# A new order by stored rules, output banks for the second batch's transform, zero fills by DMA, and the filter's sign applied once

## The chip, the cores and the metric

The kernel runs on one core of a Trainium2 chip. The metric is device time in microseconds (us) for one execution; lower is better. Times of the kernel before are the median of three runs. Engines are named as the trace does: PE is TensorE (PEld its weight loads), DVE is VectorE, ACT is ScalarE, POOL is GpSimd, SP is SyncE, which issues nearly all DMAs.

## The reference, cut to what matters

The input x has 8 batches of 3008 positions and 256 channels. Each batch is filtered in the frequency domain along its positions, and each of the 24064 resulting tokens goes through a two-layer network:

```python
X = np.fft.rfft(x, axis=1)
Y = X * (filt_r + 1j * filt_i)[None, :, :]
x = np.fft.irfft(Y, n=3008, axis=1).reshape(24064, 256)
h = x @ w_in                                  # 256 -> 2048
out = (h * (1.0 / (1.0 + np.exp(-1.702 * h)))) @ w_out   # 2048 -> 256
```

## The kernel before, in words

The transform of length 3008 = 64 x 47 is done as small matrix products: a 64-point step (`s1`), a 47-point step (`s2`), the product with the filter, and the way back (`i2`, `i1`). Values for the network are split into a rounded high half and a low half (`xh`, `xl`; `gh`, `gl`; the two halves of each weight), and three products of halves replace one.

Batch 0 is transformed by `first_fft` in plain float32; its filter rows (`f_s`, two frequency groups per DMA) are held in the tiles `f_y`, `f_o` (these in the pool `out`) and `f_buf`. The filter's imaginary part is scaled by a sign table, on ScalarE, in `filtered`. Batches 1 to 7 are transformed by `fft(b)`: `parts` splits x into halves, `s1` writes results into PSUM (kind "oz" in the output banks for the first two x tiles of batch 1), they go to memory (`a_d`), come back into the tile `zy` as z, and `forward`, `product`, `parted` and `backward` do the rest. `load_f` loads filter rows into `f_buf`; for batch 1 it loads them unsigned, scales them on ScalarE with a second sign table (`sign_sb`) and stores the signed rows to `fs` in memory, from which later batches load them.

The weights come as pairs of 32-bit words per number; `weight` turns each of 16 blocks (8 of w_in, 8 of w_out in turn) into halves with ScalarE, VectorE and GpSimd, in temporary tiles `w_tu`, over which `zy` is laid later. Token tiles 0 to 4 (512 tokens each, batch 0) are worked off in turns: `first_0` makes a first product (6 matmuls into an h bank, kind "l"), `gelu` its halves, `second_0` the second product (6 matmuls, added up in two output banks over a token tile's 16 turns). The first 32 turns go over token tiles 0 and 1 together, four turns for each pair of weight blocks. From then on, tokens are worked off in pairs of tiles, with seven products in place of eight: 7 batches of 3 pairs, 8 cycles each. `start`/`pair_signal` prepare the operands of the next pair while one is worked on.

PSUM has four banks "h" (first products, transform results) and four banks "o" (second products; transform results of kind "oz").

Nothing is issued as the code is read. The class `Planner` records every instruction with a cost in microseconds. `dues` gives each matmul a target time (the matmul costs summed in program order) and each other instruction a due time, counted back from the matmuls it feeds and from the tiles that must come free. `plan` then walks the five engines along simulated clocks: the engine whose clock is lowest takes, of what is ready and has room, the instruction with the lowest due (TensorE: the lowest target, within REACH of the lowest open one). VectorE and GpSimd exclude each other for work between SBUF tiles (`port`). The order that results is written out by hand for each engine, so that every engine works its list in that order and waits where it must. All instructions of the plan show the same line in the trace, so groups are told apart by their tiles. A tile's name there is that of the first user of its place: `half_of_xh` and `half_of_xl` are both places of the pool `half`, `tab_of_tab` becomes the pairs' c tile, `big_of_x` a tile of the pool `big`.

Places the change touches: `_tables` (sign tables), `Planner.dues`, `room`, `plan`; `nc.caps` (how many tiles of a kind are open at once); `filtered`; `load_f`, `forward` and `backward` in `fft`; and the loop over `turns` (`LEAD`, `BLANK`), which fills unused rows of `zy` and `c_buf` with zeros on GpSimd.

Of the kernel before, what the change touches and what calls it, by code (L numbers as in the profile page):

```python
# [20 lines left out]
P = 128  # L21
# [10 lines left out]
def _tables():  # L32
# [59 lines left out]
    sign_q, d_q, e_q = np.zeros((P, NG)), np.zeros((P, 2, 2, 48)), np.zeros((P, 2, 2, 48))  # L92
    row = np.arange(R).reshape(2, 2, NH)
    for u in range(2):
        h, q = slice(48 * u, 48 * u + 48), slice(64 * u, 64 * u + 48)
        sign_0[h] = sign_q[q] = sign[:, :, u]
# [11 lines left out]
    tabs = [t1_0, np.eye(P), d_0, sign_0, e_0, t2, t1_q, d_q, e_q, t2_q, sign_q]  # L108
# [125 lines left out]
class Planner:  # L234
# [7 lines left out]
    HOP, REACH, NEAR, AHEAD = 0.2, 30.0, 2.5, 50.0  # L242
# [103 lines left out]
    def dues(self):  # L346

        ops, before, lines = self.ops, {}, {}
        for n, o in enumerate(ops):
            for m in o.preds:  # L350
                ops[m].succs.append(n)
        for n, o in enumerate(ops):
# [9 lines left out]
        now, target = 0.0, {}  # L362
        for n, o in enumerate(ops):
            if o.eng == "tensor":
                target[n] = now
                now += o.cost
        for n in range(len(ops) - 1, -1, -1):
            o = ops[n]
            due = target.get(n, now + 20.0)
# [3 lines left out]
            o.due = due  # L373
        return target, now, {k: [t for t, _ in line] for k, line in lines.items()}

    def plan(self):
        ops = self.ops
        target, now, lines = self.dues()
        free = {k: {i: 0.0 for i, (_, after) in enumerate(v) if after is None} for k, v in self.sites.items()}
        turn = {k: 0 for k in lines}  # L380
        held = {k: [] for k in lines}
        left_of = {name: len(u) for name, u in self.users.items()}
        last = {}
        ready = {e: [] for e in self.ENGINES}
        clock = {e: 0.0 for e in self.ENGINES}
        port, pipe = 0.0, 0.0
        for n, o in enumerate(ops):
            o.left, o.at = len(o.preds), 0.0
            if not o.left:
                ready[o.eng].append(n)  # L390
        left, order, rank, head, done = len(ops), [], sorted(target), 0, set()
        first = {name: next((target[n] for n in u if n in target), 0.0) for name, u in self.users.items()}

        def opens(o):
            return [b for b in o.names.values() if isinstance(b, Block) and b.slot is None]

        def room(o, t):
            for b in opens(o):
                if lines[b.kind][turn[b.kind]] is not b:
                    return False  # L400
                if b.kind in self.caps and sum(last.get(k.name, 1e9) > t if not left_of[k.name] else 1 for k in held[b.kind]) >= self.caps[b.kind]:
                    return False
                if b.kind == "x" and here < 200 and o.due > here + self.AHEAD:
                    return False
                n = sum(v <= t + 1e-9 for v in free[b.pool].values())
                if b.kind == "f":
                    for k in "agbl":
                        if k in lines and turn[k] < len(lines[k]):
                            n -= first[lines[k][turn[k]].name] < here + self.NEAR
                if n < 1:  # L410
# [3 lines left out]
        while left:  # L414
            eng = min(self.ENGINES, key=lambda e: clock[e])
            t = clock[eng]
            while head < len(rank) and rank[head] in done:
                head += 1
            here = target[rank[head]] if head < len(rank) else 1e9
            best, soon, rival = None, 1e9, 1e9  # L420
            other = {"vector": "gpsimd", "gpsimd": "vector"}.get(eng)
            if other and clock[other] <= t + 1e-9:
                rival = min((ops[n].due for n in ready[other] if ops[n].port and ops[n].at <= t and room(ops[n], t)), default=1e9)
            for n in ready[eng]:
                o = ops[n]
                if o.at > t + 1e-9:
                    soon = min(soon, o.at)
                elif o.port and port > t + 1e-9:
                    soon = min(soon, port)
                elif o.port and rival < o.due:  # L430
                    soon = min(soon, t + 0.01)
                elif eng == "tensor" and target[n] > here + self.REACH:
                    pass
                else:
                    key = (target[n] if eng == "tensor" else o.due, n)
                    if (best is None or key < best[0]) and room(o, t):
                        best = key, n
            if best is None:
                clock[eng] = min(t + 0.05, soon)
                if t > 2 * now + 1000:  # L440
                    stuck = [ops[r] for q in ready.values() for r in q]
                    raise RuntimeError(f"stuck: {[(o.eng, o.call, list(o.names)) for o in stuck][:8]}")
                continue
            n = best[1]
            o = ops[n]
            ready[eng].remove(n)
            for b in opens(o):
                turn[b.kind] += 1
                b.slot = min((v, i) for i, v in free[b.pool].items())[1]
                del free[b.pool][b.slot]  # L450
                held[b.kind] = [k for k in held[b.kind] if left_of[k.name] or last[k.name] > t] + [b]
            clock[eng] = t + o.cost
            o.at, o.end = t, clock[eng] + o.extra
            if o.call == "dma_start":
                pipe = max(pipe, t + 1.5) + (o.extra - 3.2)
                o.end = pipe + 1.7
            if o.port:
                port = clock[eng]
            order.append(n)
            done.add(n)  # L460
            left -= 1
            for name, b in o.names.items():
                left_of[name] -= 1
                last[name] = max(last.get(name, 0.0), o.end)
                if isinstance(b, Block) and not left_of[name]:
                    free[b.pool][b.slot] = last[name] + self.HOP
                    for pool, i in self.opened_by.get(name, ()):
                        free[pool][i] = last[name] + self.HOP
            for m in o.succs:
                p = ops[m]  # L470
                p.left -= 1
                p.at = max(p.at, o.end + self.HOP if p.eng != eng or o.call == "dma_start" else clock[eng])
                if not p.left:
                    ready[p.eng].append(m)
        self.span = max(o.end for o in ops), now
        order.sort(key=lambda n: (ops[n].at, n))

        def real(a):
# [3 lines left out]
            return a.on(self.sites[b.pool][b.slot][0].on(b.dtype, b.name))  # L482

        for n in order:
            o = ops[n]
            getattr(getattr(self.nc, o.eng), o.call)(*map(real, o.args), **{k: real(v) for k, v in o.kw.items()})  # L486

# [10 lines left out]
def tile_kernel(  # L498
# [47 lines left out]
    nc.caps = {"first": 6, "w": 5, "ws": 2, "x": 2, "ab": 4, "raw": 4, "l": 2}  # L546
# [25 lines left out]
    sign_sb = const.tile([P, P], F32, name="sign_sb")[:, :NG]  # L572
# [124 lines left out]
    def first_fft():  # L697
# [29 lines left out]
        load_in(sign_sb, tabs[:, TAB + LATE + P :])  # L727
# [21 lines left out]
        def filtered(g):  # L749
# [5 lines left out]
            nc.scalar.activation(f[:, i, 1], f[:, i, 1], AF.Copy, scale=table["sign_0"][:R, g : g + 1])  # L755
            f_r, f_i = (f[:, i, c : c + 1].broadcast_to((R, 2, D)) for c in range(2))
# [26 lines left out]
    def fft(b):  # L783
# [80 lines left out]
        def forward(g, k):  # L864

            for u in range(2):
                ps = held(f"s2_{b}_{g}_{k}_{u}")
# [34 lines left out]
        def backward(i):  # L902
# [3 lines left out]
            for u in range(2):  # L906
                ps = held(f"i2_{b}_{i}_{u}")
# [257 lines left out]
    LEAD, NEXT, TAIL, AHEAD, BLANK = 24, 70, 20.0, 4, 28  # L1165
# [187 lines left out]
```

## Time and profile before

| what | value |
|---|---|
| median of 3 runs | 2294.06 us (2293.56 to 2294.53) |
| the profiled execution | 2293.91 us, of which the span of its instructions is 2292.1 us |
| mean granted TensorE clock | 0.995 of full |
| PE busy | 2251.4 us (98%), 10416 matmuls |
| DVE, ACT, POOL busy | 1483.2, 1638.0 and 1101.0 us (65, 71 and 48%) |
| DMA | 475.40 MB, mean 207 GB/s |

Busy time of an engine is the sum of its instructions' times; register, semaphore and DMA-issuing instructions are left out. PE is the busiest throughout, so the question at any place is what PE waits for there.

### The profile page before, as it was taken

The page shows a single profiled execution, that of the slowest core. Times are in us where ns is not written, and L with a number is a line of the kernel's source. Part 1 is how long each engine was busy: PE and PEld are TensorE (multiplying, and loading weights), DVE is VectorE, ACT ScalarE, POOL GpSimd, SP SyncE. Part 2 cuts the span into 40 slices and gives each one's busy share as a digit, 9 for nine tenths or more (in the row PEclk, how much of TensorE's full clock was granted, in tenths as well). Part 3 has the DMA queues.
Part 4 walks back from the last instruction along what each step waited for, and adds up shares of the span by engine and source line. Part 5 has one row for each costly group of instructions (what it writes and reads, how often), then busy time and mean ns, then how long its engine had stood idle before and what let it go on. Part 6 is the DMA issues. An engine that isn't in the chain of part 4 may idle for free.

```text
span 2292.1 us, 31503 instructions
## 1 busy us (share of the span) xinstructions
PE 2251.4 (98%) x10416; PEld 1866.8 (81%) x10416; DVE 1483.2 (65%) x2262; ACT 1638.0 (71%) x2939; POOL 1101.0 (48%) x941
## 2 busy tenths in 40 slices
PE   8699999999999999999999999999999999999999
PEld 8587788888888888888888888888888788888887
DVE  5857865778557874578755886457865678643433
ACT  6657967777767776677776877767777677766665
POOL 5654654565426654366453564435644456322211
PEclk9899999999999999999999999999999999999999
DMA  6736658866778568885688766887668776555443
GB/s 215 224 120 184 184 159 256 238 203 210 237 255 234 182 207 258 250 227 186 206 260 246 218 199 196 277 242 222 190 196 273 197 220 190 185 171 162 145 167 107
DMA packets 191907, 475.40 MB, mean 207 GB/s; under 512 B 19840, under 2 KB 91264, under 8 KB 191744
## 3 DMA queue, kind: packets, MB, share of 16 engines
q1 hardware_dynamic: 191600, 473.33, 67.1%
q8 instruction: 82, 1.34, 0.3%
q14 instruction: 81, 0.66, 0.1%
q10 hardware_dynamic: 144, 0.07, 0.0%
HBM read 367.94 MB, written 105.38 MB: 206 GB/s over the span
## 4 chain that ended last, share of the span: by engine, by line
PE 83%; DVE 2%; ACT 1%; issue 0%; POOL 0%; DMA 0%; POOLq 0%; ACTq 0%
PE bank_h L486 43%; PE bank_o L486 39%; DVE zy_of_zy L486 0%; DVE u_buf L486 0%; DVE tab_of_tab L486 0%; DVE big_of_x L486 0%; DMA wo_of_wo<-w 0%; ACT gh_of_gh L486 0%; DVE c_all L486 0%; POOL zy_of_zy L486 0%; DVE wi_of_br L486 0%; ACT c_all L486 0%; ACT bank_h L486 0%; DVE wo_of_wo L486 0%; ACT tab_of_tab L486 0%
## 5 line engine op out<-in xcount | busy, mean ns | idle before, releaser
L486 PE MATMUL bank_o<-wo_of_wo 128*128 128x512 f32 x2016 | 535.7, 390 | 0.0
L486 PE MATMUL bank_o<-gh_of_gh,wo_of_wo 128*128 128x512 f32 x1648 | 462.7, 392 | 3.3 <-DVE f_buf L486 3.3
L486 POOL TENSOR_TENSOR gl_of_gl<-tab_of_tab,gh_of_gh 128x512 fp32r<-128x512 f32 x168 | 218.1, 1298 | 497.4 <-ACT tab_of_tab L486 400.3
L486 PEld LDWEIGHTS bank_o<-wo_of_wo 128*128 128x128 f32 x2016 | 378.4, 188 | 77.7
L486 PE MATMUL bank_h<-y_a,wi_of_wi 128*128 128x512 f32 x1584 | 431.7, 392 | 2.1 <-DVE wo_of_wo L486 1.1
L486 PE MATMUL bank_h<-y_of_y,wi_of_wi 128*128 128x512 f32 x1464 | 415.1, 393 | 3.6 <-DVE big_of_x L486 2.5
L486 PEld LDWEIGHTS bank_o<-gh_of_gh,wo_of_wo 128*128 128x128 f32 x1648 | 309.3, 188 | 68.5 <-DVE f_buf L486 3.2
L486 PEld LDWEIGHTS bank_h<-y_a,wi_of_wi 128*128 128x128 f32 x1584 | 294.9, 188 | 65.1 <-DVE tab_of_tab L486 2.8
L486 ACT ACTIVATE bank_h<-bank_h 128x512 f32<-128x512 f32 x584 | 346.3, 593 | 0.3
L486 PEld LDWEIGHTS bank_h<-y_of_y,wi_of_wi 128*128 128x128 f32 x1464 | 273.5, 188 | 62.4 <-DVE big_of_x L486 4.0
L486 DVE TENSOR_TENSOR gl_of_gl<-bank_h,gh_of_gh 128x512 fp32r<-128x512 f32 x244 | 168.3, 690 | 214.2 <-ACT bank_h L486 208.6
L486 DVE TENSOR_TENSOR wo_of_wo<-bank_h,wo_of_wo 128x512 fp32r<-128x512 f32 x340 | 233.8, 688 | 80.5 <-ACT bank_h L486 68.0
L486 PE MATMUL bank_h<-wo_of_wo,wi_of_wi 128*128 128x512 f32 x960 | 268.6, 392 | 1.3 <-DVE tab_of_tab L486 0.7
L486 ACT ACTIVATE gh_of_gh<-bank_h 128x512 fp32r<-128x512 f32 x244 | 146.0, 598 | 168.7 <-PE bank_h L486 162.0
L486 PE MATMUL bank_o<-gl_of_gl,wo_of_wo 128*128 128x512 f32 x824 | 263.3, 393 | 1.6 <-POOL gl_of_gl L486 0.9
L486 ACT ACTIVATE wo_of_wo<-bank_h 128x512 fp32r<-128x512 f32 x340 | 201.0, 591 | 28.9 <-PE bank_o L486 15.8
L486 PEld LDWEIGHTS bank_h<-wo_of_wo,wi_of_wi 128*128 128x128 f32 x960 | 178.6, 188 | 39.3 <-DVE tab_of_tab L486 2.2
L486 ACT COPY wi_of_br<-bank_h 128x512 f32<-128x512 f32 (+1 forms) x242 | 141.8, 587 | 72.1 <-PE bank_h L486 66.6
L486 POOL TENSOR_TENSOR zy_of_zy<-u_buf,zy_of_zy 48x512 fp32r<-48x512 f32 x112 | 157.9, 1410 | 69.1 <-DVE zy_of_zy L486 58.3
L486 DVE TENSOR_TENSOR c_all<-bank_h,c_all 48x512 f32<-48x512 f32 x224 | 153.9, 687 | 48.0 <-ACT c_all L486 43.0
L486 PEld LDWEIGHTS bank_o<-gl_of_gl,wo_of_wo 128*128 128x128 f32 x824 | 154.1, 189 | 36.2 <-POOL gl_of_gl L486 3.4
L486 POOL TENSOR_TENSOR zy_of_zy<-c_buf,zy_of_zy 48x512 fp32r<-48x512 f32 x112 | 150.8, 1347 | 58.3 <-DVE zy_of_zy L486 32.9
(231 smaller groups left out, 3229.0 us busy)
## 6 DMA issues: line engine op xcount, KB each, us to landing
wi_of_wi<-w SPq DMA_DIRECT2D x168, 896.0 KB, 5.4
wo_of_wo<-w SPq DMA_DIRECT2D x168, 512.0 KB, 5.7
zy_of_zy<-a_d SPq DMA_DIRECT2D x224, 192.0 KB, 4.4
a_d<-big_of_x SPq DMA_DIRECT2D x110, 256.0 KB, 5.0
out_dram<-out_of_f_o SPq DMA_DIRECT2D x46, 512.0 KB, 6.7
f_buf<-fs SPq DMA_DIRECT2D x96, 192.0 KB, 3.5
big_of_x<-in_x_dram SPq DMA_DIRECT2D x30, 512.0 KB, 5.9
b_d<-big_of_x SPq DMA_DIRECT2D x62, 192.0 KB, 4.2
```

Source lines behind the costliest of these rows:

```text
L486: getattr(getattr(self.nc, o.eng), o.call)(*map(real, o.args), **{k: real(v) for k, v in o.kw.items()})
```

## The change

- The plan is made in steps of 25 us of simulated time. Each step has a rule from `POLICIES`: which copy of the due times is used (the plain ones or one of eight with normal noise of 1 to 8 us), NEAR and REACH. `WAYS` stores the rule of each of 91 steps, one character each; after them the plain rule goes on. The choice at each moment is as before (lowest due first).
- Due times have a further link: the users of the last four "oz" tiles come before the opening of the fourth output tile "o".
- Caps: "l" 3 instead of 2, and a new kind "of", 2.
- For batch 1, the results of `forward` and `backward` for u = 1 go to output banks (kind "of") instead of h banks.
- `filtered` stores its signed filter rows to `fs`, two groups at a time; `load_f` loads from `fs` for every batch; the scaling, the stores of batch 1 and the second sign table go.
- The unused rows 48 to 63 and 112 to 127 of `zy` are filled with zeros by two DMAs out of zero rows of `d_sb` at turn 24; the eight memsets of `zy` and the two of `c_buf` go.

```diff
-    HOP, REACH, NEAR, AHEAD = 0.2, 30.0, 2.5, 50.0
+    HOP, AHEAD, STEP, SIGMA = 0.2, 50.0, 25.0, (1.0, 1.0, 3.0, 3.0, 8.0, 1.0, 2.0, 2.0)
+    POLICIES = [(i, 2.5, 30.0) for i in range(9)] + [(i, near, reach) for i in (0, 1) for near, reach in ((1.0, 30.0), (4.0, 30.0), (2.5, 10.0), (0.0, 20.0))]
+    WAYS = "10683121a0744gg11801450a044ee55043a5e9eea200003ddee21000091eee241030ceee4e28a0013005078000"
...
+                if t.kind == "o" and len(line) == 4:
+                    for u, _ in lines.get("oz", [])[-4:]:
+                        for m in self.users[u.name]:
+                            before.setdefault(m, []).append(n)
...
+        due = np.array([o.due for o in ops])
+        rng = np.random.default_rng(0)
+        self.dues_of = [due.tolist()]
+        for sigma in self.SIGMA:
+            self.dues_of.append((due + sigma * rng.standard_normal(len(due))).tolist())
...
+        s, mark = self.ready_to_plan(), 0.0
+        for way in self.WAYS:
+            mark += self.STEP
+            self.go(s, self.POLICIES[int(way, 36)], mark)
+        assert self.go(s, self.POLICIES[0], 1e9)
+        self.emit(s)
...
-    nc.caps = {"first": 6, "w": 5, "ws": 2, "x": 2, "ab": 4, "raw": 4, "l": 2}
+    nc.caps = {"first": 6, "w": 5, "ws": 2, "x": 2, "ab": 4, "raw": 4, "l": 3, "of": 2}
...
             nc.scalar.activation(f[:, i, 1], f[:, i, 1], AF.Copy, scale=table["sign_0"][:R, g : g + 1])
+            if g % 2:
+                nc.sync.dma_start(fs[:, g - 1 : g + 1], f[:, i - 1 : i + 1])
...
             for to, of in at:
-                load_in(to, (fs if b > 1 else filt)[of])
-            if b == 1:
-                for n in range(2):
-                    m = 2 * g + n
-                    nc.scalar.activation(f[:, n, 1], f[:, n, 1], AF.Copy, scale=sign_sb[:Q, m : m + 1])
-                for to, of in at:
-                    nc.sync.dma_start(fs[of], to)
+                load_in(to, fs[of])
...
-                ps = held(f"s2_{b}_{g}_{k}_{u}")
+                ps = held(f"s2_{b}_{g}_{k}_{u}") if b > 1 or u == 0 else nc.tile("o", (P, 2, D), F32, f"s2_{b}_{g}_{k}_{u}", "of")
...
-            for c in c_buf[0:2]:
-                nc.gpsimd.memset(c[32:64], 0.0)
+            for r in (48, 112):
+                load_in(
+                    zy[0][r : r + 16].bitcast(F32).rearrange("p (n d) -> p n d", d=4 * P),
+                    d_sb[Q:, 0:4].bitcast(F32).rearrange("p a d -> p (a d)").rearrange("p (n d) -> p n d", n=1).broadcast_to((16, 8, 4 * P)),
+                )
...
-        if n >= BLANK and n - BLANK < 8:
-            r, j = divmod(n - BLANK, 4)
-            nc.gpsimd.memset(zy[0][32 + 64 * r : 64 + 64 * r, 1024 * j : 1024 * j + 1024].bitcast(F32), 0.0)
```

## Rows read from the trace of the kernel before

**Rows 1.** The page's first part: busy time, share, instructions of each engine.
```profile
PE 2251.4 (98%) x10416; PEld 1866.8 (81%) x10416; DVE 1483.2 (65%) x2262; ACT 1638.0 (71%) x2939; POOL 1101.0 (48%) x941
```

**Rows 2.** Busy time by stretch: length, then busy us (instructions) of each engine.
```profile
core 0: us, PE busy (x) PEld busy (x) DVE busy (x) ACT busy (x) POOL busy (x), PEclk, DMA share, GB/s
50.00:77.70 27.70, 24.31 (x133) 19.19 (x131) 26.49 (x41) 18.63 (x34) 16.81 (x15) 1.00 0.52 152
77.70:92.80 15.10, 0.35 (x2) 0.24 (x2) 14.74 (x18) 6.02 (x10) 9.93 (x8) 0.67 0.68 245
92.80:100.00 7.20, 4.67 (x11) 3.18 (x12) 5.88 (x8) 4.48 (x9) 5.50 (x4) 0.50 0.60 135
100.00:200.00 100.00, 99.66 (x459) 82.69 (x458) 60.23 (x108) 62.78 (x117) 49.81 (x40) 1.00 0.58 182
200.00:300.00 100.00, 95.07 (x415) 74.85 (x415) 81.79 (x121) 87.72 (x157) 64.11 (x60) 0.98 0.59 158
300.00:2250.00 1950.00, 1944.15 (x8907) 1613.73 (x8906) 1255.00 (x1909) 1404.30 (x2507) 925.42 (x776) 1.00 0.69 214
2250.00:2292.10 42.10, 37.57 (x166) 30.80 (x164) 14.03 (x21) 21.90 (x41) 5.17 (x4) 0.99 0.31 107
```

**Rows 3.** What PE waited for, whole span: us in total, times, longest.
```profile
PE bank_o L486 <- POOL half_of_xh L486: 14.7, 1, 14.7
...
PE bank_o L486 <- DVE f_buf L486: 3.3, 2, 2.5
```

**Rows 4.** POOL's timeline, 60 to 100 us: start, duration, instruction, idle before.
```profile
77.48 1.44 POOL L486 TENSOR_TENSOR wo_of_wo<-zy_of_w_tu,wo_of_wo 128x512 fp32r<-128x512 f32 x1
...
86.39 1.44 POOL L486 TENSOR_TENSOR wo_of_wo<-zy_of_w_tu,wo_of_wo 128x512 fp32r<-128x512 f32 x1
...
90.80 1.71 POOL L486 TENSOR_TENSOR half_of_xh<-out_of_f_o,half_of_xh 128x512 fp32r<-128x512 f32 x1
...
96.74 1.46 POOL L486 TENSOR_TENSOR wo_of_wo<-zy_of_w_tu,wo_of_wo 128x512 fp32r<-128x512 f32 x1
```

**Rows 5.** PE's timeline, 105 to 118 us: the first products of two turns.
```profile
109.04 1.52 PE L486 MATMUL bank_h<-y_of_y,wi_of_wi 128*128 128x512 f32 x6
...
111.76 1.52 PE L486 MATMUL bank_h<-y_of_y,wi_of_wi 128*128 128x512 f32 x6
```

**Rows 6.** POOL's timeline, 100 to 140 us: the next blocks of w_out.
```profile
112.29 1.29 POOL L486 TENSOR_TENSOR wo_of_wo<-zy_of_w_tu,wo_of_wo 128x512 fp32r<-128x512 f32 x1 [2.98 <-ACT wo_of_wo L486]
...
123.52 1.29 POOL L486 TENSOR_TENSOR wo_of_wo<-zy_of_w_tu,wo_of_wo 128x512 fp32r<-128x512 f32 x1
...
139.55 1.30 POOL L486 TENSOR_TENSOR wo_of_wo<-zy_of_w_tu,wo_of_wo 128x512 fp32r<-128x512 f32 x1 [1.49 <-ACT wo_of_wo L486]
```

**Rows 7.** What PE waited for from 100 to 300 us, the two longest.
```profile
PE bank_h L486 <- DVE big_of_x L486: 2.5, 3, 1.9
PE bank_h L486 <- DVE c_all L486: 1.7, 4, 0.7
```

**Rows 8.** Busy time of two short stretches, columns as in rows 2.
```profile
288.00:290.00 2.00, 1.94 (x5) 1.56 (x6) 1.79 (x4) 0.74 (x2) 1.43 (x1) 0.50 0.70 197
...
140.00:160.00 20.00, 20.00 (x96) 16.71 (x95) 8.38 (x21) 9.83 (x18) 13.46 (x13) 1.00 0.23 88
```

**Rows 9.** Two tiles' instructions: count, ns least/median/most, first and last start.
```profile
L486 ACT ACTIVATE f_buf<-f_buf,sign_sb x16: 492/508/511, 109.5 to 286.7; 112x256 f32<-112x256 f32 x16
...
L486 DVE COPY out_of_f_o<-bank_o x48: 425/692/693, 176.6 to 2288.0; 128x512 f32<-128x512 f32 x46, 128x256 f32<-128x256 f32 x2
```

**Rows 10.** DMA queue, 12 to 32 and 32 to 60 us: packets, MB, share.
```profile
q1 hardware_dynamic: 2281, 6.08, 103.1%
...
q1 hardware_dynamic: 1478, 2.63, 27.6%
```

**Rows 11.** POOL's timeline, whole span, its memsets: the run of eight.
```profile
142.16 7.75 POOL L486 MEMSET zy_of_zy<- 32x1024 f32 x8
```

**Rows 12.** What PE waited for from 300 us on, the longest single wait.
```profile
PE bank_h L486 <- POOL zy_of_zy L486: 1.0, 1, 1.0
```

More of the change, by code (lines that the diff above doesn't have):

```diff
@@ L351, in dues @@
                 ops[m].succs.append(n)
+            if o.eng == "tensor":
+                ideal[n] = now
+                now += o.cost
         for n, o in enumerate(ops):
@@ L372, in dues @@
                     due = min(due, ops[m].due - o.cost - o.extra - (self.HOP if ops[m].eng != o.eng else 0))
[L373 to L399, printed above, removed]
@@ new lines, in dues, with go, opens, room @@
+            o.due = due if due < 1e9 else self.last_due
+    def go(self, s, policy, mark):
+        ops, lines, target, rank = self.ops, self.lines, self.target, self.rank
+        shift, near, reach = policy
+        caps, first, ENGINES, HOP = self.caps, self.first, self.ENGINES, self.HOP
+        clock, ready, at, end, slot = s.clock, s.ready, s.at, s.end, s.slot
+        dues = self.dues_of[shift]
+        def opens(n):
+            return [b for b in self.blocks[n] if b.name not in slot]
+        def room(n, t):
+            for b in self.blocks[n]:
+                if b.name in slot:
+                    continue
+                k = b.kind
+                if lines[k][s.turn[k]] is not b:
@@ L400, in room @@
                     return False
-                if b.kind in self.caps and sum(last.get(k.name, 1e9) > t if not left_of[k.name] else 1 for k in held[b.kind]) >= self.caps[b.kind]:
+                if k in caps and sum(s.last.get(h.name, 1e9) > t if not s.left_of[h.name] else 1 for h in s.held[k]) >= caps[k]:
                     return False
-                if b.kind == "x" and here < 200 and o.due > here + self.AHEAD:
+                if k == "x" and here < 200 and dues[n] > here + self.AHEAD:
@@ L404, in room @@
                     return False
[L405 to L410, printed above, removed]
-                    return False
-            return True
-        while left:
-            eng = min(self.ENGINES, key=lambda e: clock[e])
+                m = sum(v <= t + 1e-9 for v in s.free[b.pool].values())
@@ L416, in plan @@
+                if k == "f":
+                    for j in "agbl":
+                        if j in lines and s.turn[j] < len(lines[j]):
+                            m -= first[lines[j][s.turn[j]].name] < here + near
+                if m < 1:
+                    return False
+            return True
+        idle = 0
+        while s.left:
+            eng = min(ENGINES, key=clock.__getitem__)
             t = clock[eng]
-            while head < len(rank) and rank[head] in done:
-                head += 1
@@ L431, in plan @@
                     soon = min(soon, t + 0.01)
-                elif eng == "tensor" and target[n] > here + self.REACH:
-                    pass
-                else:
[L435 to L438, printed above, removed]
+                elif eng == "tensor":
+                    if target[n] <= here + reach:
+                        todo.append((target[n], n))
+                else:
+                    todo.append((dues[n], n))
@@ L439, in plan @@
+            todo.sort()
+            n = next((n for _, n in todo if room(n, t)), None)
+            if n is None:
                 clock[eng] = min(t + 0.05, soon)
-                if t > 2 * now + 1000:
-                    stuck = [ops[r] for q in ready.values() for r in q]
-                    raise RuntimeError(f"stuck: {[(o.eng, o.call, list(o.names)) for o in stuck][:8]}")
+                idle += 1
+                if idle > 4000:
+                    return False
                 continue
-            n = best[1]
+            idle = 0
@@ L445, in plan @@
             o = ops[n]
             ready[eng].remove(n)
[L447 to L451, printed above, removed]
+            for b in opens(n):
+                s.turn[b.kind] += 1
+                free = s.free[b.pool]
+                slot[b.name] = i = min((v, i) for i, v in free.items())[1]
+                del free[i]
+                s.held[b.kind] = [k for k in s.held[b.kind] if s.left_of[k.name] or s.last[k.name] > t] + [b]
@@ L452, in plan @@
             clock[eng] = t + o.cost
-            o.at, o.end = t, clock[eng] + o.extra
+            at[n], end[n] = t, clock[eng] + o.extra
             if o.call == "dma_start":
-                pipe = max(pipe, t + 1.5) + (o.extra - 3.2)
-                o.end = pipe + 1.7
+                s.pipe = max(s.pipe, t + 1.5) + (o.extra - 3.2)
+                end[n] = s.pipe + 1.7
             if o.port:
[L458 to L461, printed above, removed]
+                s.port = clock[eng]
@@ L462, in plan @@
+            s.order.append(n)
+            s.done[n] = 1
+            s.left -= 1
+            s.work[eng] += o.cost
             for name, b in o.names.items():
[L463 to L466, printed above, removed]
+                s.left_of[name] -= 1
+                s.last[name] = max(s.last.get(name, 0.0), end[n])
+                if not s.left_of[name] and isinstance(b, Block):
+                    s.free[b.pool][slot[name]] = s.last[name] + HOP
@@ L467, in plan @@
                     for pool, i in self.opened_by.get(name, ()):
-                        free[pool][i] = last[name] + self.HOP
+                        s.free[pool][i] = s.last[name] + HOP
             for m in o.succs:
                 p = ops[m]
-                p.left -= 1
-                p.at = max(p.at, o.end + self.HOP if p.eng != eng or o.call == "dma_start" else clock[eng])
-                if not p.left:
+                s.wait[m] -= 1
+                at[m] = max(at[m], end[n] + HOP if p.eng != eng or o.call == "dma_start" else clock[eng])
@@ L474, in plan, with ready_to_plan @@
+                if not s.wait[m]:
                     ready[p.eng].append(m)
-        self.span = max(o.end for o in ops), now
-        order.sort(key=lambda n: (ops[n].at, n))
+        return True
+    def ready_to_plan(self):
+        ops = self.ops
+        self.target, now, before, self.lines = self.links()
+        self.last_due = now + 20.0
+        self.dues(self.target, before)
+        self.rank = sorted(self.target)
+        self.blocks = [[b for b in o.names.values() if isinstance(b, Block)] for o in ops]
+        self.first = {name: next((self.target[n] for n in u if n in self.target), 0.0) for name, u in self.users.items()}
+        due = np.array([o.due for o in ops])
[3 more added lines that the diff above has]
+            self.dues_of.append((due + sigma * rng.standard_normal(len(due))).tolist())
+        return State(self)
@@ L478, in real, with plan, emit @@
+    def plan(self):
+        s, mark = self.ready_to_plan(), 0.0
[4 more added lines that the diff above has]
+        self.emit(s)
+    def emit(self, best):
+        ops, at, order = self.ops, best.at, best.order
+        order.sort(key=lambda n: (at[n], n))
         def real(a):
@@ L481, in real @@
             b = a.tensor
-            return a.on(self.sites[b.pool][b.slot][0].on(b.dtype, b.name))
+            return a.on(self.sites[b.pool][best.slot[b.name]][0].on(b.dtype, b.name))
         for n in order:
@@ L486, in plan, with __init__ @@
             getattr(getattr(self.nc, o.eng), o.call)(*map(real, o.args), **{k: real(v) for k, v in o.kw.items()})
+class State:
+    def __init__(self, p):
+        ops = p.ops
+        self.free = {k: {i: 0.0 for i, (_, after) in enumerate(v) if after is None} for k, v in p.sites.items()}
+        self.turn = {k: 0 for k in p.lines}
+        self.held = {k: [] for k in p.lines}
+        self.left_of = {name: len(u) for name, u in p.users.items()}
+        self.last, self.slot = {}, {}
+        self.ready = {e: [] for e in p.ENGINES}
+        self.clock = {e: 0.0 for e in p.ENGINES}
+        self.port, self.pipe, self.work = 0.0, 0.0, {e: 0.0 for e in p.ENGINES}
+        self.wait = [len(o.preds) for o in ops]
+        self.at, self.end = [0.0] * len(ops), [0.0] * len(ops)
+        self.done, self.left, self.head, self.order = bytearray(len(ops)), len(ops), 0, []
+        for n, o in enumerate(ops):
+            if not self.wait[n]:
+                self.ready[o.eng].append(n)
 class Stream:
```

48 lines of the change are left out of this document (25 added, 23 removed).

## The prediction

> **What bounds the kernel now.** I read the page's first part, then the busy time by stretch, then who TensorE waited for, and last the timelines of the worst stretch. The first shows TensorE busy for 2251.4 of 2292.1 us [rows 1]: no edit changes what it has to multiply, so only its 40.7 us of idle and its stretches at half clock can be won. The second shows where they lie [rows 2]. From 300 to 2250 us only 5.85 us of 1950 are idle, and the last 42.1 us hold 4.53 (the last product's tail). The loss is at the start: 3.39 us idle from 50 to 77.7, 14.75 from 77.7 to 92.8, 2.53 from 92.8 to 100, 4.93 from 200 to 300. After the long gap the granted clock is 0.50, which is 1.2 of 2.4 GHz, and the 4.67 us of work to 100 us cost 2.34 us more than at full clock. So the stretch from 77.7 to 100 us loses 14.75 + 2.53 + 2.34 = 19.6 us.
>
> The waits name it [rows 3]: one wait of 14.7 us for a GpSimd write to `half_of_xh`, then f_buf. The write is the low half of the second batch's second x tile, issued by `parts`. GpSimd began it at 90.80, behind the conversion of weights (77.48 and 86.39 are two of those) [rows 4], and TensorE went on as it ended. Behind that matmul, in TensorE's written order, stand the second products of the first token tiles: until this transform result is copied out, it holds one of the four output banks, and the two token tiles of the first turns need all four. The f_buf wait is that copy. So one late low half blocks the turns, though their weights are there.
>
> **The change, part by part.** The sum starts from the profiled execution's own 2293.91 us (span 2292.1 and 1.8 around it), 0.15 below the median 2294.06.
>
> *The order, first 100 us.* New is a link in the due times: every user of the last four "oz" tiles (transform results in output banks, their copies among them) is now due before the fourth output tile opens. Beside it `l` goes from 2 to 3, so one more first product may wait for its gelu. And the plan runs in steps of 25 us, each with one of 17 rules (noise on the due times, NEAR, REACH); the first hundred microseconds have rules 1, 0, 6, 8. If the low half comes before the weights, what is late next? The weights. Four turns use one pair of weight blocks; a turn takes 2.72 us (109.04 to 111.76) [rows 5], so a pair lasts 10.9. The second block of a pair is complete (start plus duration) at 78.92, 87.83 and 98.20 [rows 4], then at 113.58, 124.81 and 140.85 [rows 6]. Walking on from 77.7: wait 1.2; work to 89.8, 100.7, 111.6; wait 2.0, to 124.5; wait 0.3, to 135.7; wait 5.1. That is 8.6 us of new waits, so 19.6 - 8.6 = 11.0 are won if weights come when they do now. GpSimd is busy 49.8 of 100 us from 100 to 200 [rows 2], so they could come earlier: at best only the first 1.2 remain, 18.4 won. At worst the low half is late again: 0, or as much as the gap once more in another place. I take 11.0, the end worked out from the present arrivals.
>
> *Second transform in output banks too.* Half of `forward`'s and `backward`'s results (u = 1) of the second batch go to "of" tiles, at most two. Today they share the four h banks with the first products, and from 100 to 300 us TensorE waits 2.5 us for `big_of_x` and 1.7 for `c_all` [rows 7], both copies of such results. Gain at most the 4.93 idle plus half of the 1.94 us that ran at 0.50 [rows 8]: 5.9. Against it: a token tile that opens its output banks may now find them held. There are three such changes (tile 2 to 3, 3 to 4, 4 to the pairs), each worth one copy, 0.69 us by VectorE [rows 9], behind another, say 1.3: 3.9 lost at worst. I take the two named waits, 4.2 won.
>
> *Sign once.* Gone are 16 ScalarE scalings of 0.508 us, 8.1 us in all [rows 9], 16 stores and the load of the sign table; the filter is now stored signed from the first batch, eight stores of 96 x 4 KB. ScalarE is busy 87.7 of 100 us from 200 to 300 [rows 2], and its share of the relief is in the 4.2 above. The eight stores go into SP's queue in the first 50 us, ahead of loads of weights and x. Together 3.1 MB; the queue moves 6.08 MB in the 20 us from 12 to 32 and is full there (103%), so they are worth 10.3 us of queue. From 32 to 60 it is used to 27.6% [rows 10], 20 us free. I charge nothing, since that cover is twice the need; without it every weight pair is up to 10.3 us later and TensorE pays that. The x loads into the `out` tiles now also wait for two of these stores to land; their first matmuls wait for the split table anyway.
>
> The Trainium skill (DMA: Bandwidth & Descriptors, "Issuing engines are not separate DMA queues") says that all transfers end up on the same 16 engines and interleave. By that rule the stores are no free filler, they slow the weight loads around them; the sum with all of it uncovered would be 10.3 us higher. The full queue from 12 to 32 us agrees, the free one after it limits it.
>
> *Zero fills.* Eight GpSimd memsets, 7.75 us in one run from 142.16 [rows 11], become two DMAs of zeros (16 rows of 16 KB each); two short ones vanish. TensorE is busy for all 20 us from 140 to 160 [rows 8]: nothing won. The DMAs must land before the second transform reads z: I charge nothing, TensorE having its turns meanwhile; a late one delays that transform once, by at most the 10.3 us of a full queue.
>
> *The other 1990 us.* Their work is the same, their order is newly chosen. Idle there is 5.85 us before the tail, so no more can be won; I take 0.
>
> Sum: 2293.91 - 11.0 - 4.2 = 2278.7, so 2279. Its own range is 2271 (7.4 more, weights earlier) to 2286.
>
> **The rivals.**
> *A. The gap stays or moves.* For: GpSimd took the low half after the weight blocks although x had long landed, and the shared rules of choice are the old ones; the link adds mostly to the copies, and the low half's due time was early before. VectorE is busy 26.5 of 27.7 us from 50 to 77.7 [rows 2], so the stretch has little slack for any order. Against: the copies are what holds the banks, and a step that stalls TensorE is what a choice among rules would avoid. Time: only the banks' part, 2293.91 - 4.2 = 2289.7, with a spread of 4.
> *B. Slower: the hand-overs.* 21 times (7 batches of 3) the signal of the next pair must be finished by GpSimd and VectorE just before its first product. Now the longest wait after 300 us is one of 1.0 [rows 12]; the rest are below it. Rules with noisy due times, kept for 25 us each, may make the last split late at each: 21 x 1.0 = 21 us. With the start's gain kept, 2278.7 + 21 = 2299.7; it is slower than before from 0.73 us a hand-over on. For: the plan's clock knows no queueing of DMAs beyond one pipe, and an order that is tight there has nothing left on the chip. Against: the present order, made by the same clock, loses next to nothing.
> *C. Nothing of it acts.* The noise is small and ties decide, so the order stays in essence: 2293.9 within 3.
>
> **How the numbers follow.** Forecast 0.57, A 0.20, B 0.15, C 0.08. What this kernel's measurement can tell from no change is 0.2%, 4.6 us: faster is below 2289.5, slower above 2298.6. Forecast gives faster 0.56, same 0.01; A is split evenly, 0.10 faster and 0.09 same, 0.01 slower; B gives 0.02, 0.02, 0.11; C 0.01, 0.05, 0.02. That is 0.69, 0.17 and 0.14; I shift 0.04 to slower for mishaps not listed: 0.66, 0.16, 0.18. The range goes from 2264 (most of the 18.4 and of the banks' 5.9) to 2298, up to B's lower half.
>
> **What would show it.** Right: no wait of TensorE over 5 us between 60 and 100 us, the low half of x done before the weight blocks, a granted clock of 1.00 there, and less than 2 us idle from 200 to 300. The weights' part is right if small waits for wi and wo stand at 110 to 145. Wrong: a wait of over 10 us for any x half or f_buf (A); more than 15 us idle from 300 to 2250, spread over the hand-overs (B); weight loads of the first 32 us that land some 10 us later than now (the stores).

## The result, and the profile after

The changed kernel takes 2260.82 us (median of 4 runs, 2260.01 to 2261.07) against 2293.81 for the kernel before, taken with it: ratio 0.9856, 95% interval 0.9839 to 0.9873. That is 33 us, where 15 were forecast; it lies 3 us below the range's low end.

The first part of the page after answers to [rows 1]:

```profile
PE 2240.7 (99%) x10416; PEld 1864.8 (83%) x10416; DVE 1469.7 (65%) x2262; ACT 1626.6 (72%) x2923; POOL 1093.2 (48%) x931
```

The number of matmuls is the same. Busy time by stretch, the stretches of [rows 2] up to 300 us:

```profile
50.00:77.70 27.70, 26.82 (x148) 21.57 (x147) 25.38 (x38) 20.14 (x38) 19.02 (x14) 1.00 0.64 191
77.70:92.80 15.10, 15.10 (x69) 12.49 (x68) 13.46 (x21) 11.03 (x21) 7.63 (x6) 1.00 0.58 200
92.80:100.00 7.20, 7.20 (x33) 5.99 (x32) 4.52 (x9) 4.55 (x9) 3.68 (x3) 1.00 0.53 178
100.00:200.00 100.00, 98.74 (x462) 81.74 (x462) 69.43 (x118) 69.49 (x127) 48.49 (x40) 1.00 0.64 179
200.00:300.00 100.00, 98.47 (x453) 79.96 (x452) 79.78 (x121) 82.80 (x150) 65.28 (x61) 1.00 0.54 150
```

From 77.7 to 100 us TensorE never rests, at a granted clock of 1.00; 19.6 us were lost there. From 50 to 77.7 it rests 0.88 us (3.39 before), from 200 to 300 it rests 1.53 (4.93 before, and about 1.6 more were lost at half clock from 288 to 292 us). On GpSimd, the low halves of x now stand ahead of all weight blocks but the first (59.57); answering to [rows 4] and [rows 6], its timeline from 50 us:

```profile
53.22 2.51 POOL L524 TENSOR_TENSOR half_of_xl<-out_of_f_o,half_of_xh 128x512 fp32r<-128x512 f32 x2
55.77 2.60 POOL L524 TENSOR_TENSOR half_of_xh<-out_of_f_o,half_of_xl 128x512 fp32r<-128x512 f32 x1
...
59.57 1.29 POOL L524 TENSOR_TENSOR wi_of_wi<-zy_of_w_tu,wi_of_wi 128x512 fp32r<-128x512 f32 x1
60.81 1.32 POOL L524 TENSOR_TENSOR half_of_xh<-out_of_f_o,half_of_xl 128x512 fp32r<-128x512 f32 x1
...
64.12 1.47 POOL L524 TENSOR_TENSOR wo_of_wo<-zy_of_w_tu,wo_of_wo 128x512 fp32r<-128x512 f32 x1
...
75.79 1.53 POOL L524 TENSOR_TENSOR wo_of_wo<-zy_of_w_tu,wo_of_wo 128x512 fp32r<-128x512 f32 x1 [1.30 <-ACT wo_of_wo L524]
...
87.25 1.52 POOL L524 TENSOR_TENSOR wo_of_wo<-zy_of_w_tu,wo_of_wo 128x512 fp32r<-128x512 f32 x1 [1.30 <-ACT wo_of_wo L524]
...
98.94 1.29 POOL L524 TENSOR_TENSOR wo_of_wo<-zy_of_w_tu,wo_of_wo 128x512 fp32r<-128x512 f32 x1 [3.52 <-ACT wo_of_wo L524]
...
108.49 1.81 POOL L524 TENSOR_TENSOR wo_of_wo<-zy_of_w_tu,wo_of_wo 128x512 fp32r<-128x512 f32 x1 [1.37 <-ACT wo_of_wo L524]
...
122.23 1.28 POOL L524 TENSOR_TENSOR wo_of_wo<-zy_of_w_tu,wo_of_wo 128x512 fp32r<-128x512 f32 x1
...
133.89 1.29 POOL L524 TENSOR_TENSOR wo_of_wo<-zy_of_w_tu,wo_of_wo 128x512 fp32r<-128x512 f32 x1
```

What came at 90.80 is done by 62.1, and the weights lose little by it. The second blocks of the pairs that the prediction walked along end at 77.3, 88.8, 100.2, 110.3, 123.5 and 135.2, where it had 78.9, 87.8, 98.2, 113.6, 124.8 and 140.9: the second and third 0.9 and 2.0 us later, the others 1.3 to 5.7 us earlier. TensorE's waits for weight blocks from 50 to 200 us (total, times, longest):

```profile
PE bank_h L524 <- ACT wi_of_wi L524: 0.3, 1, 0.3
```

Where else did time go? To compare equal work I use two marks of the SP timeline: the first store of the first pair's tokens (451.65 before, 425.87 after) and the first store of the last pair but one (2208.85 and 2175.15). Between them both kernels run 8019 matmuls, and from the second mark to the end of the span it takes 83.25 us in both. The span is 33.7 us shorter (2292.1 and 2258.4). So 25.8 us are won ahead of the first mark, and 33.7 - 25.8 = 7.9 between the marks, in work that the change does not touch. Before:

```profile
451.65:2208.85 1757.20, 1751.65 (x8019) 1453.62 (x8019) 1149.20 (x1744) 1271.64 (x2268) 846.20 (x711) 1.00 0.69 214
```

and after:

```profile
425.87:2175.15 1749.28, 1746.77 (x8019) 1454.14 (x8019) 1143.53 (x1745) 1270.15 (x2267) 845.08 (x711) 1.00 0.69 215
```

The idle between them fell only from 5.55 to 2.51 us, 3.0 of the 7.9. The other 4.9 stood in the busy column: the same 8019 matmuls count 1751.65 and then 1746.77. A matmul is shown as 0.39 us long, but in a run the next begins 0.227 us later (1.52 us for six), so about the first 0.16 us of every wait hides under the modelled end of the last matmul. The waits at the weight loads show more: 16.5 us in all before and 7.1 after, 9.4 less, somewhat over the 7.9 that were won. Between the marks, the four longest of ten groups before (us in total, times, longest):

```profile
PEld bank_h L486 <- DVE tab_of_tab L486: 5.0, 9, 0.6
PEld bank_h L486 <- DVE wo_of_wo L486: 3.8, 5, 1.0
PEld bank_o L486 <- POOL gl_of_gl L486: 3.4, 6, 1.2
PEld bank_h L486 <- POOL zy_of_zy L486: 1.5, 1, 1.5
```

and after, all there are:

```profile
PEld bank_h L524 <- DVE tab_of_tab L524: 3.1, 5, 0.9
PEld bank_h L524 <- DVE wo_of_wo L524: 2.6, 4, 0.9
PEld bank_h L524 <- DVE big_of_x L524: 1.4, 2, 0.9
```

### The profile page after: what moved, and what is told of

Its sections match the earlier page's. It is cut to its first block, busy times and chain, and to the rows that moved or that the text cites. A ratio compares the mean times of both kernels' runs of the same rounds, so it can differ in the third digit from the quotient of the medians.

```text
span 2258.4 us, 31563 instructions
## 1 busy us (share of the span) xinstructions
PE 2240.7 (99%) x10416; PEld 1864.8 (83%) x10416; DVE 1469.7 (65%) x2262; ACT 1626.6 (72%) x2923; POOL 1093.2 (48%) x931
## 5 line engine op out<-in xcount | busy, mean ns | idle before, releaser
L524 PE MATMUL bank_o<-wo_of_wo 128*128 128x512 f32 x2016 | 542.7, 390 | 0.0
L524 ACT COPY wi_of_t<-bank_h 128x512 f32<-128x512 f32 (+1 forms) x217 | 127.4, 587 | 87.1 <-PE bank_h L524 85.1
L524 POOL TENSOR_TENSOR zy_of_zy<-u_buf,zy_of_zy 48x512 fp32r<-48x512 f32 x112 | 152.9, 1365 | 72.5 <-DVE zy_of_zy L524 54.4
L524 DVE TENSOR_TENSOR c_all<-bank_h,c_all 48x512 f32<-48x512 f32 x208 | 142.4, 687 | 45.5 <-ACT c_all L524 42.0
```

## The experiments

Times are medians; the ratios of the numbered runs are to the kernel before on the same chip (2295.0 to 2295.6 there). The stored string has 90 characters, not the 91 that earlier parts speak of. "First mark" and "between" are as above.

| run | us | ratio (95%) | first mark | between |
|---|---|---|---|---|
| before | 2293.81 | 1 | 451.65 | 1757.2 |
| changed | 2260.82 | 0.9856 (0.9839-0.9873) | 425.87 | 1749.3 |
| 1 half first | 2286.16 | 0.9954 (0.9936-0.9972) | 442.48 | 1757.1 |
| 2 banks | 2276.31 | 0.9913 (0.9897-0.9930) | 433.90 | 1757.3 |
| 3 less work | 2281.33 | 0.9934 (0.9916-0.9952) | 438.35 | 1756.7 |
| 4 rules to 400 us | 2268.25 | 0.9879 (0.9861-0.9897) | 424.49 | 1758.5 |
| 5 one rule | 2268.26 | 0.9880 (0.9866-0.9895) | 430.10 | 1752.1 |
| 6 one rule, no "of" | 2269.31 | 0.9889 (0.9874-0.9903) | 431.34 | 1752.3 |
| 7 noisy rule | 2293.12 | 0.9991 (0.9982-1.0001) | 445.27 | 1762.9 |
| 8 rules chosen anew | 2253.55 | 0.9817 (0.9802-0.9831) | 421.96 | 1747.2 |
| 9 sign only | 2285.98 | 0.9959 (0.9945-0.9972) | 439.36 | 1761.0 |
| 10 l 3 only | 2286.38 | 0.9962 (0.9948-0.9975) | 442.22 | 1761.4 |
| 11 changed again | 2258.96 | 0.9840 (0.9826-0.9853) | 425.06 | 1749.4 |
| 12 as 8, again | 2253.51 | 0.9819 (0.9806-0.9832) | 421.50 | 1747.2 |

Runs 1 to 4 were on one chip, runs 5 to 8 on a second, runs 9 to 12 on a third. The stretch of runs 4 and 9 between the marks holds 5 and 10 matmuls more than the others' 8019 or 8020, 1.1 and 2.3 us of work.

**1. The low half first.**
```diff
             o.due = due
+            if any(name.startswith(("xh_1_0", "xl_1_0", "xh_1_1", "xl_1_1")) for name in o.names):
+                o.due = -50.0
```


> The kernel before, with one thing changed in the planner: the splits of the first two x tiles of batch 1 get the earliest due time of all, so GpSimd takes their low halves as soon as they can be made. Everything else, work, banks and caps, stays. Theory order (the gap is only the low half standing behind the weight blocks on GpSimd): the 14.7 us wait goes, the stretch from 77.7 to 100 us loses less than 4 us, and the time is 2294 less 11 to 18, so 2276 to 2283; losses from 200 us on stay as before. Rival banks (the first turns lack PSUM room, the half is only where it shows): the gap turns up elsewhere before 130 us and the time stays at 2290 or above.

The long wait is gone: TensorE waits 0.4 us for an x half, and the loss from 50 to 100 us falls from 23.1 to 6.3 (4.76 idle, 1.56 by the clock). What is late next is what the prediction named, the weights (waits of TensorE from 50 to 200 us):

```profile
PE bank_o L488 <- POOL wo_of_wo L488: 2.4, 3, 1.2
PE bank_o L488 <- ACT wo_of_wo L488: 1.3, 3, 0.5
...
PE bank_o L488 <- POOL half_of_xh L488: 0.4, 1, 0.4
```

9.2 us are won by the first mark. That is close to the 11.0 of the prediction, but partly by luck: the waits for weight blocks are 3.7 us (2.4 and 1.3), not 8.6, and the stretch from 300 to 450 us, which was to stay as before, now rests 2.9 us in place of 0.3. The time is 3 us above the expectation's upper end (9.5 us under the kernel before on its chip, 11 to 18 expected). The order caused the gap; moving the half alone does not give the whole 19.6 back.

**2. Caps and output banks alone.**
```diff
-    nc.caps = {..., "l": 2}
+    nc.caps = {..., "l": 3, "of": 2}
-                ps = held(f"s2_{b}_{g}_{k}_{u}")
+                ps = held(f"s2_{b}_{g}_{k}_{u}") if b > 1 or u == 0 else nc.tile("o", (P, 2, D), F32, f"s2_{b}_{g}_{k}_{u}", "of")
...
```


> The kernel before with the caps and banks of the change alone: l 3 instead of 2 and the second batch's u = 1 results in output banks. Rule of choice, link, sign, stores and memsets as before. Theory order: longer chains through held banks are what made the weights due early; with more room their due times fall behind those of the x halves, the gap closes (under 2 us lost from 77.7 to 100) and the 200 to 300 us stretch loses under 3 us instead of 6.4: 2266 to 2274. Rival rules (the stored rules close the gap): the 200 to 300 us stretch improves by 3 to 4 us, the gap stays above 8 us, time 2286 to 2291.

17.8 us are won by the first mark (25.8 in the changed kernel), with no stored rule and no link. The gap closes (2.2 us idle from 50 to 100), and 200 to 300 us rests 2.1. But 300 to 450 us now rests 6.0 us, where before it was 0.3, so the time is 2 us above the expectation:

```profile
50.00:100.00 50.00, 47.77 (x242) 39.56 (x242) 41.65 (x68) 35.82 (x67) 27.55 (x23) 1.00 0.66 200
...
300.00:450.00 150.00, 144.03 (x655) 116.52 (x654) 91.23 (x153) 105.76 (x190) 83.91 (x69) 1.00 0.83 254
```

The due times explain why the gap closes. `dues` counts back through held tiles (a tile's users are due before the opener of the tile that takes its place), and with two "l" tiles and one chain of "f" tiles that chain is longer than the matmuls' own time. Worked out from the kernels' code, the last low half of the two x tiles is due at 51.6 simulated us in the kernel before, in this run and in the changed kernel. In the kernel before, the low halves of seven weight blocks are due ahead of it (19.8 to 47.1). With the caps and banks of this run, and in the changed kernel, none is (52.0 and later). Each engine works its written list, so this is the order on the chip: in this run GpSimd has made that half by 60.1 us. The caps also change when a tile may open; no run parts the two effects.

**3. The removed work alone.**
```diff
 (filtered, load_f and the zero fills as in the change; caps, banks, rule and due times as before)
```


> The kernel before with the removed work alone: sign applied once and stored from batch 0, zero fills by two DMAs, the table and the memsets gone; banks, caps and the rule of choice as before, no link. Theory hidden (the removed work lay beside TensorE's): within 4 us of before, 2290 to 2296, the gap of 14 us still there. Rival draw (the gap is an accident of one order, and any edit that changes the order a little removes it): the gap is under 5 us, 2275 to 2282. The eight stores of the signed filter cost nothing if the first 50 us lose 4 to 5 us as before, and up to 10 us more if they hold up the weights.

The rival had it: 13.3 us by the first mark, although the rule and the caps are the old ones. The low half still comes behind weights, as the due times are those of the kernel before, but at 75.99 us in place of 90.80. The first 50 us rest 4.37 us (4.34 before): the eight stores cost nothing.

**4. Stored rules for 400 us only.**
```diff
-    WAYS = "10683121a0744gg11801450a044ee55043a5e9eea200003ddee21000091eee241030ceee4e28a0013005078000"
+    WAYS = "10683121a0744gg1"
```


> The changed kernel with the stored rules for its first 16 steps (400 us) only, the plain rule after them. The first 400 us are the same order. Theory rules (what the changed kernel gained from 450 us on, some 8 us, comes from the chosen rules): 2267 to 2271, the 8 us lost between 450 us and the end. Rival (the steady part gained by work removed or by the hand-over from the first 400 us): 2259 to 2263.

The first 400 us are as in the changed kernel, and between the marks the whole 7.9 us are lost again (1758.5, or 1757.4 for equal work):

```profile
424.49:2183.03 1758.54, 1752.30 (x8024) 1454.21 (x8024) 1147.36 (x1746) 1274.22 (x2271) 846.28 (x711) 1.00 0.70 214
```

So the steady part was won by the rules of choice and by nothing else in the change.

**5 and 6. One rule, with and without the output banks.**
```diff
-    WAYS = "10683121a0744gg1..."
+    WAYS = "a" * 91          # run 5: NEAR 4.0; run 6 also takes "of" out of forward and backward
```


> The changed kernel with one rule for all 91 steps: the plain due times, REACH 30, NEAR 4.0 in place of 2.5. Nothing is chosen per step. Theory rules (the stored string earns some 8 us in the first 400 us and 8 after): 2272 to 2278. Rival NEAR (one wider NEAR would have done it, the string is hardly needed): 2261 to 2268, of which the part after 450 us loses at most 3 us against the changed kernel.

> As the run with one rule (NEAR 4.0 throughout), but the second batch's u = 1 results go to the h banks again; l stays at 3. Theory banks (the output banks relieve the stretch from 100 to 300 us, as the prediction had it, about 4 us): 3 to 8 us slower than the one-rule run, lost between 50 and 300 us. Rival (the banks matter through the due times alone, and the token tiles' openings pay for them): within 2 us of the one-rule run.

Run 5 lies at the upper end of its rival: the change with one wider NEAR, nothing chosen, gets 26.8 us (2295.03 to 2268.26) of the 33 to 36 that the changed kernel gets, and 5 of the 8 between the marks:

```profile
430.10:2182.16 1752.06, 1748.31 (x8019) 1453.58 (x8019) 1130.89 (x1745) 1268.69 (x2268) 847.74 (x711) 1.00 0.69 214
```

Beyond it, the string is worth 6 to 9 us by the ratios (0.9880 against 0.9856 and 0.9840); in the traces it is 4.2 by the first mark and 2.8 between. Run 6 is the same as run 5 within its interval, and 1.2 us later at the first mark. In detail the output banks do relieve the stretch that the prediction had in mind (50 to 300 us rests 4.8 us with them, 7.8 without), but 300 to 450 us pays: it rests 4.6 with them and 1.1 without. What the banks relieve there is largely paid later.

**7. A rule with much noise.**
```diff
+    WAYS = "5" * 91          # due times with normal noise of 8 us
```


> The changed kernel with one rule for all steps, the one with the largest noise on the due times (normal, 8 us). Theory handovers (the slower rival of the prediction: noisy due times bring waits at the hand-overs all along): 15 to 30 us are lost after 300 us against the changed kernel, the time is 2285 to 2305, and the waits stand on the signal's splits. Rival (due times have slack, noise is harmless): 2262 to 2272.

Between the marks 13.6 us are lost against the changed kernel (5.7 against the kernel before), and ahead of the first 19.4. The time is inside the expectation, and the 13.6, with 2.6 us more rest from 300 us to the first mark, reach the low end of its 15 to 30. But the place is not the one expected: TensorE waits for the gelu's low halves (`gl`, and `wo`, where `gl` tiles lie later) and for the sums in the c tile (`tab`), not for the signal's splits. The three longest groups of waits at the weight loads between 445 and 2208 us:

```profile
PEld bank_o L524 <- POOL gl_of_gl L524: 7.2, 10, 1.6
PEld bank_h L524 <- DVE wo_of_wo L524: 3.0, 3, 1.3
PEld bank_h L524 <- DVE tab_of_tab L524: 2.5, 6, 1.0
```

**8, 11 and 12. The first rules chosen anew.** For each step the 17 rules were tried from the 24 best states so far, and those kept whose planned order had begun the most matrix work by the end of the step.
```diff
-    WAYS = "10683121a0744gg11801450a..."
+    WAYS = "40183108a48240g01801450a..."
```


> The changed kernel with its first 16 stored rules chosen anew, for the most matrix work begun at the end of each step by the planner's own clock; the other 75 rules stay. Theory (the planner's clock ranks orders as the chip does): what the changed kernel still loses from 200 to 450 us, about 3.5 us, shrinks to under 1.5, the time is 2257 to 2260. Rival (at this size the clock no longer ranks): 2260 to 2264 or more, losses only moved.

> The changed kernel once more, beside the others on one chip: 2259 to 2263, ratio 0.984 to 0.987, so that the run with its first 16 rules chosen anew (ratio 0.9817) is faster by 5 to 9 us beyond what chips differ by. If chips or days differ by that much, 2254 to 2258 would come out here.

> The kernel with its first 16 rules chosen anew, on the same chip as the changed one: 2252 to 2256 and 5 to 9 us under it. If the first result was the chip's, it comes within 2 us of it.

On one chip 2253.51 against 2258.96, 5.5 us faster than the changed kernel, which was itself 2 us better there than in the first result; this version beats both. Run 8 came out 3.5 us under the low end that was expected, runs 11 and 12 as expected. From 200 to 300 us TensorE never rests any more, and little from 300 to 450 (run 12); from 100 to 200 us it rests 2.9 (1.8 in run 11):

```profile
200.00:300.00 100.00, 100.00 (x465) 82.91 (x464) 81.04 (x126) 84.01 (x150) 62.05 (x58) 1.00 0.56 159
300.00:450.00 150.00, 149.79 (x698) 124.81 (x697) 102.30 (x162) 112.06 (x201) 86.69 (x72) 1.00 0.83 252
```

The first mark came 3.6 us earlier than in run 11, and another 2.2 were won between the marks, though no rule there was changed. Over all twelve kernels, the simulated clock of the planner, which needs no chip, puts the end of the plan between 2248 us (run 8) and 2304 (run 7), where the chip has 2254 to 2294. It has the kernels in nearly the measured order and spreads them wider.

**9 and 10. The sign alone, and the cap alone.**
```diff
 (run 9: filtered stores, load_f loads from fs, its scalings and stores gone)
 (run 10:)
-    nc.caps = {..., "l": 2}
+    nc.caps = {..., "l": 3}
```


> The kernel before with the sign alone applied once: batch 0 stores its signed filter rows, batch 1 loads them, its 16 scalings and 16 stores go; memsets, banks, caps and rule stay (the second sign table is still loaded). Theory draw (every edit gives a new order, and what it wins or loses is a draw of where that order waits): the gap from 77.7 to 100 us shrinks below 8 us, but another stretch before 450 us loses more than before, 2284 to 2293. Rival sign (ScalarE's 8 us are what the first batches wait for): the stretch from 200 to 300 us loses under 3 us, nothing else is worse, 2276 to 2283.

> The kernel before with one more first product open (l 3 instead of 2), nothing else. Theory l (the chain through two held products is what makes the weights due before the x halves): the 14.7 us wait falls below 6 us and 2278 to 2285 results, the stretch from 200 to 300 us losing as much as before, over 5 us. Rival of (the output banks of the second batch do both): 2290 or above.

Run 9 went as the draw has it: 50 to 100 us rests 4.5 in place of 20.7, and 300 to 450 us rests 5.4 in place of 0.3. Run 10 won 9.4 us by the first mark (its expectation's upper end missed by 1.4); the low half comes at 74.92 (six weight blocks are still due ahead of it), and other waits stand in the same stretch (3.1 us for the split table, 2.1 for f_buf). Between the marks its trace is 4.2 us longer than the kernel before; it is of an execution 2.9 us over the run's median, so how much of that is the order's stays open.

The stretch from 50 to 100 us lost 23.1 us in the kernel before (idle, and what the half clock cost). It loses 6.3, 2.2, 6.5 and 4.5 us in runs 1, 2, 3 and 9, and 13.1 in run 10. So four different edits each closed most of one gap, a fifth a good part of it, and their gains do not add up.

## Why the prediction was right or wrong

- **Where the time lies, and what PE waits for:** right for the start. The low half behind the weights was the gap (run 1), and the signs named for it came: no long wait from 60 to 100 us, a granted clock of 1.00 there, 1.53 us of rest from 200 to 300.
- **The order of the first 100 us, 11.0 us:** the direction was right, the size is the first failing term. All 19.6 us came back, and 2.5 more from 50 to 77.7 that were not in the sum. What failed is the walk: 8.6 us of new waits for weights, where 0.3 were measured. It kept the present arrivals, and the blocks from the fourth on come 1.3 to 5.7 us earlier; over the new arrivals the same walk gives 3.1. It also let TensorE do nothing but whole turns, four to a pair, where the trace has first products of the next turns, matmuls of the second batch's transform and of the next signal ahead of the late blocks. So the sign named for this part, small waits for wi and wo at 110 to 145 us, did not come. Run 1, where only the half moved, has 3.7 us of such waits.
- **The link** was taken for the cause. It is not: the changed kernel's planner writes the same order for every engine with the link and without it, so the kernel is the same. The caps and the second batch's banks alone close the gap (run 2), and the rules win the steady part (run 4).
- **Second transform in output banks, 4.2 us:** the two named waits are gone, and 200 to 300 us loses 5.0 us less (its half clock cost 1.6 us, not 0.97: the 1.94 us of [rows 8] were only part of it). But runs 5 and 6 show no gain of the banks clear of noise under one rule: 1.2 us by the first mark, with 3.0 us less rest before 300 us and 3.5 more after. So the size fits the stretch, not the part that it was put down to; the banks act through the order.
- **Sign once, zero fills, 0:** their own work was beside TensorE, as costed: 20.00 of 20 us busy from 140 to 160 in both, and the queue is used to 51.4% from 32 to 60 us. As edits they were not neutral, since each draws a new order (runs 3 and 9). Of the 10.3 us of the case without cover, nothing came: the first 50 us rest 4.69 us (4.34 before), but all of that difference stands before the first matmul (4.26 us in place of 3.91), and the first of the eight stores is issued at 28.2. The median landing of the w_in loads issued from 12 to 32 us rose from 6.7 to 7.8 us, and TensorE did not wait for it. That transfers share 16 engines and interleave whichever engine starts them, as the Trainium skill says (DMA: Bandwidth & Descriptors, "Issuing engines are not separate DMA queues"), agrees with these later landings.
- **The other 1990 us, 0:** the second failing term, and the step as put was wrong: "no more can be won" than 5.85 us of idle. 7.9 were won, because the idle column hides part of each wait, and the rules won them (run 4). Even within the 5.85, the 0 was taken without a reason.
- **Rivals:** A and C fell. Noise in the due times does cost (run 7, 13.6 us between the marks), but not at the hand-overs, where B had put it, and the stored string does not behave like such a draw: between the marks it is 13.6 us better than that one. The prediction treated it as noise. How the string was found is not on record.
- **The range:** its low end, 2264, has no sum behind it. The two best cases that it names give 2293.9 - 18.4 - 5.9 = 2269.6, so the result lies 9 us under what the prediction could derive, not 3.

The step that put the result outside the range is the sum of these two: 19.6 + 2.5 in place of 11.0, and 7.9 in place of 0. With them the prediction's 15.2 becomes 34.2; the profiled executions differ by 33.3.

The kernels hold a second estimate that the prediction did not use. The planner is part of both, and its simulated clock ends the two plans at 2299.0 and 2252.7 us: 46 us apart, where the prediction had 15 and 33 were measured.

What stays open: how much of the changed kernel's first 25.8 us belongs to each edit. Under one order each is a draw; runs 1 to 3, 9 and 10 won 9.2, 17.8, 13.3, 12.3 and 9.4 by themselves. No run has the changed kernel with the plain rule from the start, since the planner finds no order for it. The kernel before with NEAR 4.0 and nothing else was not run either; by the planner's clock its plan would end 7.4 us sooner, with the gap still there.

## What to carry to other kernels

Where a planner writes the order, an edit's own cost says little: the edit draws a new order, and the gaps of the old one are what it can win. So sum all stalls, at full size, as the upper end, and ask for each whether the waiting work had been ready. Read waits at the weight loads, or as time over an equal count of matmuls, not as idle of the matmuls. And where the measured times follow a planner's own clock, ask that clock first: it ranks orders before anything runs, and choosing among many by it adds to what a hand-made rule gives (here 6 to 9 us to 26.8, and 5.5 more with the first rules chosen anew).

## What the runs showed of the hardware that was not expected

The chip followed small differences between orders closely: five rounds told 2253.5 from 2259.0 us, and the same kernel's stretch between the marks came out as 1749.3 and 1749.4 us, or 1747.2 twice, on different runs. Whole times repeat less well, and ratios no better: the kernel before took 2293.8 us beside the first result and 2295.0 to 2295.6 on the three chips of the runs, and the changed kernel's ratio was 0.9856 and then 0.9840, 3.7 us apart where its times differ by 1.9.
